# VectorE's score blocks move from matmuls of their own into the third bank of the score tiles

## The chip, the cores and the metric

The kernel runs on one core of one Trainium2 chip. TensorE (PE) multiplies matrices and writes only into PSUM, ScalarE (ACT) and VectorE (DVE) read PSUM and SBUF, GpSimd (POOL) copies a few small tiles, and SyncE (SP) issues DMAs. The metric is the device time of one execution in microseconds; the time of a kernel is the median of several executions. In addition one execution is profiled, and all rows quoted here come from such an execution.

## The reference

The kernel computes a gated sum of an attention block and a dense block over the same 2048 rows of 640 numbers:

```python
def _A_ref(x, wqkv, wo):            # H = 32 heads of Dh = 20
    qkv = (x @ wqkv).reshape(B, S, 3, H, Dh) ...
    scores = jnp.einsum("bhqd,bhkd->bhqk", q, k) * Dh ** -0.5
    p = softmax(scores, axis=-1)
    o = jnp.einsum("bhqk,bhkd->bhqd", p, v)
    return o.reshape(B, S, D) @ wo
def _B_ref(x, w1, b1, w2):          # F = 1536
    h = x @ w1 + b1
    return (h * jnp.tanh(softplus(h))) @ w2
g = sigmoid((x * gate_w).sum(-1, keepdims=True))
return g * _A_ref(x, ...) + (1 - g) * _B_ref(x, ...)
```

The large part is the exponential of 32 x 2048 x 2048 scores.

## The kernel before

**Units, groups, iterations.** Four heads and 512 queries form a group; there are 32 groups. A group has 16 blocks of 128 keys, and a block of one head is a unit: one matmul with 32 rows of contraction (20 are used) gives a tile of 128 keys x 512 queries, which is one PSUM bank. The four heads `t` of a unit row lie in four different strips of 32 rows of the array (`tile_position=(32 * t, 0)`). The list `units` is cut into iterations of three and two units in turn (`WIDTHS = (3, 2)`). An iteration has a PSUM tile, `S0` with three banks or `S1` with two, and each of them exists once: the scores of iteration i + 2 go into the tile that iteration i's exponential has read.

**One iteration.** `emit_qk` (line 1056 on) issues the score matmuls (line 1070), `emit_exp` one exponential on ScalarE over all banks of the tile (line 1081), `emit_pv` the sets of four matmuls that multiply finished exponentials with V and add up in the tile `acc` (line 1128). The scores of iteration i + 1 are issued ahead of the exponential of iteration i.

**Work beside it.** All other matmuls (projections of Q, K and V, both layers of the dense block, the output projection) are cut into "chains". A chain takes one of two further PSUM banks, the pool `pp`, runs its matmuls between the score bursts, and VectorE then copies the bank out (an eviction). `pump` chooses how many matmuls of chains fit between two bursts. It follows a planner's clock for every engine (the dictionary `T`), due times, and an estimate of TensorE's recent activity: where the estimate is below `FLOOR = 0.54` and a pool bank is free, it issues a matmul on constant data (`busy`, line 1014), which keeps TensorE occupied. The order of each engine's instructions is thereby fixed when the program is built.

**VectorE's share of the exponential.** In groups 4 to 30 the last block of keys (`JV`, block 15) is not among the units: VectorE computes its exponential by integer and polynomial steps. Four chains per group, one for each head `t`, come into the pool about 2 to 11 iterations after the group's start. Each has a single matmul (line 702), and its eviction (line 711) rounds 128 x 512 scores to 16-bit integers in `E_dve`. After the fourth, `jv_steps` computes on all four heads at once: seven instructions on 128 x 2048 elements (lines 730 to 752), each issued when the planner finds room on VectorE (`run_slow`). When they are done by the planner's clock, `emit_jv` issues the set of four matmuls that adds this block to `acc`.

ScalarE also computes 48 exponentials of 128 x 512 for the dense block (line 522). SyncE's and GpSimd's queues carry loads of weights and the outputs; none of them is issued by the chains that the change touches.

Of the kernel before, what the change touches and what calls it, by code (L numbers as in the profile page):

```python
# [9 lines left out]
P = 128  # L10
ACT = mybir.ActivationFunctionType
ALU = mybir.AluOpType
# [138 lines left out]
def kernel(  # L151
# [12 lines left out]
    nc = tc.nc  # L164
    _, S, D = A_x.shape
# [6 lines left out]
    QC = 512  # L172
# [6 lines left out]
    WIDTHS = (3, 2)  # L179
    JV_GROUPS = list(range(4, 31))  # L180
    JV_BIAS = 32
    LEAD_JV = 24
    N_CAP = 1.0e9
    NCELL = 48
    CELLS_KEPT = 2
# [41 lines left out]
    F16, I16 = mybir.dt.float16, mybir.dt.int16  # L227
    E_dve = consts.tile([P, 4, QC], BF16, tag="E_dve")
    w_dve = consts.tile([P, 4, QC], F16, tag="w_dve")
    VB = consts.tile([P, H, DH + 1], BF16, tag="VB")  # L230
    u_dve = consts.tile([P, 4, QC], F16, tag="u_dve")
# [39 lines left out]
    for c in range(1, NQC):  # L271
        nc.gpsimd.dma_start(  # L272
            out=xs[c][:, :, :],
# [5 lines left out]
        out=wv[:, :, GC : GC + 1], in_=gate_w.rearrange("(kt p o) -> p kt o", p=P, o=1)  # L279
# [16 lines left out]
    groups = [(p, qc) for p in range(NQ - 2) for qc in range(NQC)]  # L296
# [5 lines left out]
    JV = NS - 1  # L302
    with_jv = [G in JV_GROUPS for G in range(len(groups))]
# [5 lines left out]
        for t in range(4)  # L309
    ]  # L310
    unit_at = {(G, j): k for k, (G, _, _, j, t) in enumerate(units) if t == 0}
    iters = []
    pos = 0
    while pos < len(units):
        n = min(WIDTHS[len(iters) % len(WIDTHS)], len(units) - pos)
        iters.append((pos, n))
        pos += n
    NI = len(iters)
    it_of = [0] * len(units)
    for i, (a, n) in enumerate(iters):  # L320
# [3 lines left out]
    def it_at(G, j=0):  # L324
        return it_of[unit_at[(G, j)]] if G < len(groups) else NI

    kT = {}
    qT = {}
    OT = {}
    Bt = {}  # L330
    act = {}
# [12 lines left out]
    now = [0]  # L344
# [3 lines left out]
    T = dict(act=0.0, pe=0.0, dve=0.0, acc=0.0)  # L348
# [3 lines left out]
    NS_SEEN = 250.0  # L352
# [4 lines left out]
    def vec(ns, dep=0.0):  # L357
        T["dve"] = max(T["dve"], dep) + ns

    def evac(ns):  # L360

        run_slow(T["pe"] + NS_SEEN + 150.0)
        vec(ns, T["pe"] + NS_SEEN)
        bank_free[-1] = max(bank_free[-1], T["dve"] + 60.0)
# [31 lines left out]
    def steps(start, parts, deadline):  # L396


        seq[0] += 1
        slow.append([deadline, seq[0], start, deque(parts)])  # L400

    def run_slow(limit):

        while True:
            todo = [x for x in slow if max(T["dve"], x[2]) + x[3][0][0] <= limit]
            if not todo:
                break
            x = min(todo, key=lambda x: x[:2])
            ns, fn = x[3].popleft()
            vec(ns, x[2])  # L410
            fn()
            if not x[3]:
                slow.remove(x)
# [29 lines left out]
    def opener(box, *shape):  # L443
        def bank():
            if "ps" not in box:
                n = shape[0] * (shape[1] if len(shape) > 1 else 1)
                box["flat"] = take_bank()[:, 0:n]
                box["ps"] = box["flat"]
                if len(shape) > 1:
                    box["ps"] = box["flat"].rearrange("p (a b) -> p a b", b=shape[1])  # L450
            return box["flat"]

        return bank
# [238 lines left out]
    ROUND = 1.5 * 2.0**23  # L692
    jv_free = [True]
    jv_at = {}

    def jv_chain(G, p, t, start, due):
        box = {}
        bank = opener(box, QC)

        def piece():  # L700
            jv_free[0] = False
            nc.tensor.matmul(  # L702
                bank()[:, :],
                lhsT=kT[p][32 * t : 32 * t + 32, JV * P : (JV + 1) * P],
                rhs=qT[G][32 * t : 32 * t + 32, :],
                tile_position=(32 * t, 0),
            )

        def finish():
            evac(690)  # L710
            nc.vector.tensor_scalar(  # L711
                out=E_dve.bitcast(I16)[:, t, :], in0=box["ps"][:, :], scalar1=ROUND,
                scalar2=ROUND - 512.0 * JV_BIAS, op0=ALU.add, op1=ALU.subtract,
            )
            if t == 3:
                left = (it_at(G + 1) - now[0]) * 1115.0
                steps(T["dve"], jv_steps(G), T["act"] + left - 4000.0)

        def ready():
            return G in qT and (jv_free[0] if t == 0 else not jv_free[0])  # L720

        return Chain(start, due, [(215, piece)], finish, ready, hard=False, bank=bank, lead=LEAD_JV)

    def jv_steps(G):
        V = nc.vector
        E, w, u = (t.rearrange("p a n -> p (a n)") for t in (E_dve, w_dve, u_dve))
        e, wi = E.bitcast(I16), w.bitcast(I16)

        def mantissa():
            V.tensor_scalar(  # L730
                out=wi, in0=e, scalar1=511, scalar2=0x4000, op0=ALU.bitwise_and, op1=ALU.bitwise_or
            )

        def exponent():
            V.tensor_scalar(
                out=e, in0=e, scalar1=-512, scalar2=2, op0=ALU.bitwise_and, op1=ALU.logical_shift_right
            )

        def square():
            V.tensor_tensor(out=w, in0=w, in1=w, op=ALU.mult)  # L740

        def factor():
            V.tensor_scalar(out=u, in0=w, scalar1=EXP_A, scalar2=EXP_C, op0=ALU.add, op1=ALU.mult)

        def factor2():
            V.tensor_scalar(out=w, in0=w, scalar1=EXP_B, scalar2=None, op0=ALU.add)

        def product():
            V.tensor_tensor(out=w.bitcast(BF16), in0=w, in1=u, op=ALU.mult)

        def scale():
            V.tensor_tensor(out=e, in0=e, in1=wi, op=ALU.add)
            jv_at[G] = T["dve"] + NS_SEEN

        return [
            (700, mantissa), (700, exponent), (1230, square), (700, factor), (700, factor2),
            (1230, product), (1230, scale),
        ]


# [126 lines left out]
    for a in range(0, NS, 4):  # L887
        chains.append(
            v_chain(list(range(a, a + 4)), wv0, 0, 4 * DH, 0, 0, max(1, it_at(0, a)))
        )  # L890

    for G, (p, qc) in enumerate(groups):
        if with_jv[G]:
            for t in range(4):
                x = it_at(G) + 1 + 2 * t
                chains.append(jv_chain(G, p, t, x, x + 2))

    def spread(a, b, n):
        return [(a + (b - a) * k / n, a + (b - a) * (k + 1) / n) for k in range(n)]
# [152 lines left out]
    E_of = {}  # L1052
    S_free = {}
    S_full = {}
    E_full = {}
    late = [0.0]

    def emit_qk(i):
        a, n = iters[i]
        w = WIDTHS[i % len(WIDTHS)]  # L1060
        tag = f"S{i % len(WIDTHS)}"
        ps = spool.tile([P, w * QC], F32, tag=tag, name="Sp")
        S_of[i] = ps
        T["pe"] = max(T["pe"], S_free.get(tag, 0.0))
        S_full[i] = T["pe"] + NS_SCORES_SEEN
        worked(T["pe"], 215.0, 0.5)
        T["pe"] += NS_SCORES
        for k in range(n):
            G, p, qc, j, t = units[a + k]
            nc.tensor.matmul(  # L1070
                ps[:, k * QC : (k + 1) * QC],
                lhsT=kT[p][32 * t : 32 * t + 32, j * P : (j + 1) * P],
                rhs=qT[G][32 * t : 32 * t + 32, :],
                tile_position=(32 * t, 0),
            )

    def emit_exp(i):
        a, n = iters[i]
        which = i % len(WIDTHS)
        E = ep[which].tile([P, WIDTHS[which] * QC], BF16, tag=f"E{which}", name="E")  # L1080
        nc.scalar.activation(  # L1081
            E[:, 0 : n * QC], S_of.pop(i)[:, 0 : n * QC], ACT.Exp, scale=LN2 / 512.0
        )
        late[0] += max(0.0, S_full[i] - T["act"])
        T["act"] = max(T["act"], S_full.pop(i)) + NS_EXP[n]
        S_free[f"S{i % len(WIDTHS)}"] = T["act"] + NS_EXP_SEEN
        for k in range(n):
            E_of[a + k] = E[:, k * QC : (k + 1) * QC]
            E_full[a + k] = T["act"] + NS_EXP_SEEN
# [33 lines left out]
    def emit_set(G, p, qc, j, moving, full, VB=None):  # L1123
        n = pv_sets[0]
        T["pe"] = max(T["pe"], full, T["acc"] if n == 0 else 0.0) + NS_SET
        worked(T["pe"] - NS_SET, 215.0, 1.1)
        for t in range(4):
            nc.tensor.matmul(  # L1128
                acc[32 * t : 32 * t + DH + 1, :],
                lhsT=VA[:, j, 4 * p + t, :] if VB is None else VB[:, 4 * p + t, :],  # L1130
                rhs=moving(t),
                start=(n == 0),
                stop=(n == NS - 1),
                tile_position=(0, 32 * t),
            )
        pv_sets[0] = n + 1
        if n == NS - 1:
            normalise(G, p, qc)
            pv_sets[0] = 0
            jv_in[0] = False  # L1140

    def emit_jv(G, p, qc):
        jv_in[0] = jv_free[0] = True
        emit_set(G, p, qc, JV, lambda t: E_dve[:, t, :], jv_at[G], VB)

    def emit_pv(limit):
        count = 0
# [193 lines left out]
```

## Time and profile before

| | |
|---|---|
| median of 3 executions | 945.32 us (940.99 to 949.07) |
| the profiled execution | 954.2 us, of which the span of all instructions is 952.3 us |
| ScalarE busy | 912.2 us, 96% of the span |
| TensorE busy | 863.2 us, 91% |
| VectorE busy | 694.3 us, 73% |
| score matmuls (line 1070), exponentials (line 1081) | 1940, 776 |
| matmuls and evictions of VectorE's blocks (lines 702, 711) | 108 each |
| matmuls on constant data (line 1014) | 246 |
| granted TensorE clock, mean | 0.962 |

A line of the profile names the source line, the engine, the operation, what is written and what is read, how often, then the busy time of the group, the mean length of one, and the idle time of the engine just before it with the instruction that ended it. An instruction's length includes the time it takes to pass through the engine, so two instructions in a row overlap; how much an engine takes per instruction is read from the distance of the starts. "Granted clock" is the share of TensorE's full clock in that stretch; here it is 1 or 0.5.

### The profile page before, as it was taken

How to read it: one execution, taken by the hardware profiler on the slowest of the kernel's cores; microseconds unless marked ns; L12 is line 12 of the kernel's file. 1: busy time of each engine (PE TensorE's matmuls, PEld its weight loads, DVE VectorE, ACT ScalarE, POOL GpSimd, SP SyncE). 2: the span in 40 equal slices, each digit the busy share in tenths (PEclk: the TensorE clock that was granted, in tenths of full speed). 3: DMA queues.
4: the chain of work that ended last, by engine and by line, in shares of the span. 5: the costliest groups of instructions: out<-in, count | busy, mean ns of one | idle time of the engine just before them, and what ended most of it. 6: DMA issues, size and time to landing. Idle time of an engine off the chain costs nothing.

```text
span 952.3 us, 14757 instructions
## 1 busy us (share of the span) xinstructions
PE 863.2 (91%) x6073; PEld 298.8 (31%) x6073; DVE 694.3 (73%) x1156; ACT 912.2 (96%) x830; POOL 21.7 (2%) x35
## 2 busy tenths in 40 slices
PE   8999989999998888899899989898999899999996
PEld 4443322222233232322223222232223223333332
DVE  4335487777888888777788988788787877876533
ACT  6999998989999999989999999999999989999995
POOL 5000010000000000000000000000000000000000
PEclk9999997979999999979999999999999989999998
DMA  9000010000100010001011001010000000000100
GB/s 289 8 1 1 21 30 1 18 4 1 31 4 19 2 30 1 21 1 50 1 30 35 22 1 30 1 50 1 21 1 21 1 1 15 35 15 9 42 28 30
DMA packets 25632, 21.96 MB, mean 23 GB/s; under 512 B 10089, under 2 KB 24313, under 8 KB 25561
## 3 DMA queue, kind: packets, MB, share of 16 engines
q1 hardware_dynamic: 22808, 14.28, 5.5%
q0 software_dynamic: 1520, 5.94, 2.0%
q8 instruction: 48, 0.79, 0.3%
q10 hardware_dynamic: 1232, 0.76, 0.3%
q14 instruction: 24, 0.19, 0.1%
HBM read 15.73 MB, written 5.24 MB: 22 GB/s over the span
## 4 chain that ended last, share of the span: by engine, by line
ACT 61%; issue 18%; PE 18%; DVE 1%; DMA 1%; POOL 1%; ACTq 0%; POOLq 0%
ACT E L1081 58%; PE Sp L1070 5%; PE acc L1128 3%; ACT e L522 3%; PE ps L657 2%; PE ps L612 2%; PE ps L581 2%; PE ps L464 2%; DMA wv<-in_A_wqkv_dram 1%; PE ps L702 1%; PE ps L1014 0%; PE ps L492 0%; DVE ot L1291 0%; DVE h L592 0%; POOL xs L272 0%
## 5 line engine op out<-in xcount | busy, mean ns | idle before, releaser
L1081 ACT ACTIVATE E<-Sp 128x1536 bf16<-128x1536 f32 (+1 forms) x776 | 894.5, 1351 | 21.9 <-PE Sp L1070 20.8
L1070 PE MATMUL Sp<-qT,kT 32*128 32x512 bf16 x1940 | 313.2, 392 | 76.6 <-ACT E L1081 65.5
L1070 PEld LDWEIGHTS <-kT 32*128 32x128 bf16 x1940 | 104.0, 91 | 306.4 <-issue 287.9
L1128 PE MATMUL acc<-E,VA 128*21 128x512 bf16 x1940 | 196.6, 395 | 0.8 <-DVE T L1096 0.8
L1128 PEld LDWEIGHTS <-VA 128*21 128x21 bf16 x1940 | 47.8, 89 | 113.0 <-issue 112.7
L711 DVE TENSOR_SCALAR E_dve<-ps 128x512 int16<-128x512 f32 x108 | 71.8, 678 | 12.7 <-PE ps L702 12.3
L581 PE MATMUL ps<-xT,w1t 128*128 128x512 bf16 x240 | 80.3, 406 | 0.0
L1014 PE MATMUL ps<-busy 128*128 128x512 bf16 x246 | 75.5, 389 | 0.0
L612 PE MATMUL ps<-w_sb,cell 128*128 128x320 bf16 x384 | 75.3, 307 | 0.0
L592 DVE TENSOR_SCALAR h<-ps,b1f 128x512 f32<-128x512 f32 x48 | 35.8, 746 | 37.5 <-PE ps L581 37.2
L464 PE MATMUL ps<-xT,wkp 128*128 128x512 bf16 x155 | 49.1, 405 | 1.7 <-DVE xT L430 0.8
L464 PE MATMUL ps<-xT,wqp 128*128 128x512 bf16 x155 | 48.4, 392 | 0.0
L657 PE MATMUL ps<-wo_sb,cell 128*128 128x320 bf16 x248 | 46.9, 305 | 0.0
L544 DVE RECIPROCAL r<-r 128x128 f32<-128x128 f32 x48 | 45.4, 945 | 1.0
L479 DVE CAST kT<-ps 128x512 bf16<-128x512 f32 x31 | 21.4, 690 | 32.2 <-PE ps L464 32.1
L475 DVE TENSOR_SCALAR qT<-ps 128x512 bf16<-128x512 f32 x31 | 21.4, 692 | 27.1 <-PE ps L464 26.9
L612 PEld LDWEIGHTS <-cell 128*128 128x128 bf16 x384 | 30.0, 98 | 34.3 <-issue 27.6
L1096 DVE STREAM_TRANSPOSE T<-acc 128x512 f32<-128x512 f32 x32 | 22.9, 715 | 23.0 <-PE acc L1128 22.8
L702 PE MATMUL ps<-qT,kT 32*128 32x512 bf16 x108 | 38.3, 387 | 0.0
L522 ACT ACTIVATE e<-h 128x512 f32<-128x512 f32 x48 | 35.5, 739 | 0.7 <-DVE h L592 0.7
L505 DVE CAST VA<-ps 128x80 bf16<-128x80 f32 (+2 forms) x48 | 16.4, 378 | 25.0 <-PE ps L492 24.9
L553 DVE TENSOR_TENSOR e<-e,r 128x512 f32<-128x512 f32 x48 | 33.2, 692 | 1.6
(107 smaller groups left out, 694.3 us busy)
## 6 DMA issues: line engine op xcount, KB each, us to landing
w1t<-in_B_w_dram SPq DMA_DIRECT2D x14, 480.0 KB, 3.7
b_dram<-Bt SPq DMA_DIRECT2D x4, 640.0 KB, 3.1
out_dram<-ot SPq DMA_DIRECT2D x14, 160.0 KB, 1.8
xs<-in_A_x_dram POOLq DMA_DIRECT2D x3, 640.0 KB, 6.7
w_sb<-in_B_w_dram POOLq DMA_DIRECT2D x1, 1920.0 KB, 12.6
ws<-in_A_wqkv_dram SPq DMA_DIRECT2D x13, 100.0 KB, 3.9
w1t<-in_B_w_dram POOLq DMA_DIRECT2D x2, 480.0 KB, 8.8
wo_sb<-in_A_wo_dram SPq DMA_DIRECT2D x4, 200.0 KB
```

The source lines that it names most:

```text
L464: nc.tensor.matmul(box["ps"][:, :], lhsT=wpad[:, kt, :, :].rearrange("p h d -> p (h d)"), rhs=xT[:, kt, chunk * QC : (chunk + 1) * QC], st ...
L522: nc.scalar.activation(e[:, :], h[:, :], ACT.Exp)
L544: V.reciprocal(out=r[:, Q], in_=r[:, Q])
L581: nc.tensor.matmul(box["ps"][:, :], lhsT=w1t[4 * c + ft // 3][:, kt, (ft % 3) * P : (ft % 3 + 1) * P], rhs=xT[:, kt, c * QC : (c + 1) * QC ...
L612: nc.tensor.matmul(box["ps"][:, :], lhsT=act[(ft, c)][:, u * P : (u + 1) * P], rhs=w2_sb[:, ft, half * HALF : (half + 1) * HALF], start=(f ...
L657: nc.tensor.matmul(box["ps"][:, :], lhsT=OT[(p, c)][:, u * P : (u + 1) * P], rhs=wo_sb[0][:, p, cols], start=(k == 0), stop=(k == len(ps_l ...
L702: nc.tensor.matmul(bank()[:, :], lhsT=kT[p][32 * t : 32 * t + 32, JV * P : (JV + 1) * P], rhs=qT[G][32 * t : 32 * t + 32, :], tile_positio ...
L711: nc.vector.tensor_scalar(out=E_dve.bitcast(I16)[:, t, :], in0=box["ps"][:, :], scalar1=ROUND, scalar2=ROUND - 512.0 * JV_BIAS, op0=ALU.ad ...
L1014: nc.tensor.matmul(ps[:, 0:n], lhsT=busy[:, :], rhs=busy_row(n), start=True, stop=True)
L1070: nc.tensor.matmul(ps[:, k * QC : (k + 1) * QC], lhsT=kT[p][32 * t : 32 * t + 32, j * P : (j + 1) * P], rhs=qT[G][32 * t : 32 * t + 32, :] ...
L1081: nc.scalar.activation(E[:, 0 : n * QC], S_of.pop(i)[:, 0 : n * QC], ACT.Exp, scale=LN2 / 512.0)
L1128: nc.tensor.matmul(acc[32 * t : 32 * t + DH + 1, :], lhsT=VA[:, j, 4 * p + t, :] if VB is None else VB[:, 4 * p + t, :], rhs=moving(t), st ...
```

## The change

VectorE's blocks lose their chains and their pool banks. When the list of units is cut into iterations, four iterations of each group 4 to 30 that would have three units get two, and the third bank of their `S0` tile takes a block of VectorE's (`extra`). The first comes at least 4 iterations after the group's start, the others 2, 4 and 2 iterations later (`JV_GAPS`). `emit_qk` issues that matmul as the third of the burst and directly behind it, through `jv_read`, VectorE's rounding read of this bank. `emit_exp` covers the first two banks. The planner's clock lets `S0` come free only when both the exponential and VectorE's read are through. A 3-bank iteration takes the head whose strip of the array is not used by its two units if one is left.

The steps of VectorE's exponential are issued twice per group, each time on 128 x 1024 elements: after the second and after the fourth read. The set that adds the block to `acc` comes when both halves are done.

```diff
-    LEAD_JV = 24
+    JV_GAPS = (4, 2, 4, 2)
...
+        x = None
+        got = taken_by.setdefault(G, [])
+        if with_jv[G] and n == 3 and len(got) < 4:
+            since = i - (got[-1][0] if got else iters_start.get(G, i))
+            if since >= JV_GAPS[len(got)] and units[pos + 1][0] == G:
+                mine = {units[pos][4], units[pos + 1][4]}
+                left = [t for t in range(4) if t not in [y for _, y in got]]
+                t = min(left, key=lambda t: (t in mine, t))
+                got.append((i, t))
+                x = (G, units[pos][1], t, len(got) - 1)
+                n = 2
...
-    def jv_chain(G, p, t, start, due):
...
+    def jv_read(G, t, slot, ps, full):
+        assert jv_free[0] or slot > 0
+        jv_free[0] = False
+        jv_slot[t] = slot
+        run_slow(full + 100.0)
+        vec(690, full)
+        nc.vector.tensor_scalar(
+            out=E_dve.bitcast(I16)[:, slot, :], in0=ps, scalar1=ROUND,
+            scalar2=ROUND - 512.0 * JV_BIAS, op0=ALU.add, op1=ALU.subtract,
+        )
+        if slot % 2 == 1:
+            left = (it_at(G + 1) - now[0]) * 1115.0
+            steps(T["dve"], jv_steps(G, slot // 2), T["act"] + left - 4000.0)
...
-            (700, mantissa), (700, exponent), (1230, square), (700, factor), (700, factor2),
-            (1230, product), (1230, scale),
+            (380, mantissa), (380, exponent), (640, square), (380, factor), (380, factor2),
+            (640, product), (640, scale),
...
-    for G, (p, qc) in enumerate(groups):
-        if with_jv[G]:
-            for t in range(4):
-                x = it_at(G) + 1 + 2 * t
-                chains.append(jv_chain(G, p, t, x, x + 2))
...
+        todo = [(units[a + k][0], units[a + k][1], units[a + k][3], units[a + k][4]) for k in range(n)]
+        if extra[i] is not None:
+            G, p, t, slot = extra[i]
+            todo.append((G, p, JV, t))
+        for k, (G, p, j, t) in enumerate(todo):
             nc.tensor.matmul(
                 ps[:, k * QC : (k + 1) * QC],
...
+        if extra[i] is not None:
+            jv_read(G, t, slot, ps[:, n * QC : (n + 1) * QC], S_full[i])
+            S_read[i] = T["dve"] + 60.0
...
+        if i in S_read:
+            S_free[tag] = max(S_free[tag], S_read.pop(i))
```

More of the change, by code (lines that the diff above doesn't have):

```diff
@@ L312 @@
     iters = []
+    extra = []
     pos = 0
+    taken_by, iters_start = {}, {}
     while pos < len(units):
-        n = min(WIDTHS[len(iters) % len(WIDTHS)], len(units) - pos)
+        i = len(iters)
+        G = units[pos][0]
+        n = min(WIDTHS[i % len(WIDTHS)], len(units) - pos)
+        x = None
[9 more added lines that the diff above has]
+                n = 2
+        for k in range(pos, pos + n):
+            iters_start.setdefault(units[k][0], i)
         iters.append((pos, n))
+        extra.append(x)
         pos += n
+    assert all(len(taken_by[G]) == 4 for G in JV_GROUPS)
     NI = len(iters)
@@ L694, with jv_steps @@
     jv_at = {}
-    def jv_chain(G, p, t, start, due):
[L697 to L724, printed above, removed]
+    jv_slot = {}
+    halves = {}
+    def jv_read(G, t, slot, ps, full):
[11 more added lines that the diff above has]
+            steps(T["dve"], jv_steps(G, slot // 2), T["act"] + left - 4000.0)
+    def jv_steps(G, half):
         V = nc.vector
-        E, w, u = (t.rearrange("p a n -> p (a n)") for t in (E_dve, w_dve, u_dve))
+        E, w, u = (
+            t[:, 2 * half : 2 * half + 2, :].rearrange("p a n -> p (a n)")
+            for t in (E_dve, w_dve, u_dve)
+        )
         e, wi = E.bitcast(I16), w.bitcast(I16)
@@ L752, in scale @@
             V.tensor_tensor(out=e, in0=e, in1=wi, op=ALU.add)
-            jv_at[G] = T["dve"] + NS_SEEN
+            halves[G] = halves.get(G, 0) + 1
+            if halves[G] == 2:
+                jv_at[G] = T["dve"] + NS_SEEN
         return [
-            (700, mantissa), (700, exponent), (1230, square), (700, factor), (700, factor2),
-            (1230, product), (1230, scale),
+            (380, mantissa), (380, exponent), (640, square), (380, factor), (380, factor2),
+            (640, product), (640, scale),
         ]
@@ L1054 @@
     S_full = {}
+    S_read = {}
     E_full = {}
@@ L1067, in emit_qk @@
         T["pe"] += NS_SCORES
-        for k in range(n):
-            G, p, qc, j, t = units[a + k]
+        todo = [(units[a + k][0], units[a + k][1], units[a + k][3], units[a + k][4]) for k in range(n)]
[3 more added lines that the diff above has]
+        for k, (G, p, j, t) in enumerate(todo):
             nc.tensor.matmul(
@@ L1085, in emit_exp @@
         T["act"] = max(T["act"], S_full.pop(i)) + NS_EXP[n]
-        S_free[f"S{i % len(WIDTHS)}"] = T["act"] + NS_EXP_SEEN
+        tag = f"S{i % len(WIDTHS)}"
+        S_free[tag] = T["act"] + NS_EXP_SEEN
+        if i in S_read:
+            S_free[tag] = max(S_free[tag], S_read.pop(i))
         for k in range(n):
@@ L1143, in emit_jv @@
         jv_in[0] = jv_free[0] = True
-        emit_set(G, p, qc, JV, lambda t: E_dve[:, t, :], jv_at[G], VB)
+        emit_set(G, p, qc, JV, lambda t: E_dve[:, jv_slot[t], :], jv_at[G], VB)
     def emit_pv(limit):
```

## The prediction, on record before the changed kernel ran

> **What bounds the kernel now.** I read the page first: busy times, granted clock, costliest groups.
>
> ```profile
> PE 863.2 (91%) x6073; PEld 298.8 (31%) x6073; DVE 694.3 (73%) x1156; ACT 912.2 (96%) x830; POOL 21.7 (2%) x35
> ...
> PEclk9999997979999999979999999999999989999998
> ...
> L1070 PE MATMUL Sp<-qT,kT 32*128 32x512 bf16 x1940 | 313.2, 392 | 76.6 <-ACT E L1081 65.5
> ...
> L711 DVE TENSOR_SCALAR E_dve<-ps 128x512 int16<-128x512 f32 x108 | 71.8, 678 | 12.7 <-PE ps L702 12.3
> ```
>
> ScalarE is busy 96% of the span. TensorE's score matmuls wait 65.5 us for ScalarE to release their tile. VectorE's eviction of a block takes 678 ns. The clock has dents. Next, the groups with shapes kept apart:
>
> ```profile
> L1081 ACT ACTIVATE E<-Sp 128x1536 bf16<-128x1536 f32 x388 | 607.8, 1567 | 6.4 <-PE Sp L1070 5.8
> L1081 ACT ACTIVATE E<-Sp 128x1024 bf16<-128x1024 f32 x388 | 440.6, 1136 | 15.5 <-PE Sp L1070 15.0
> ```
>
> These lengths overlap. In the trace's starts, the instruction after a three-bank exponential comes 1330 ns later, after a two-bank one 904, after one for the dense block 519 (each both minimum and median). So 388 x 1.330 + 388 x 0.904 + 48 x 0.519 = 891.7 us of the span is ScalarE at its rate. The first exponential starts at 10.4 us, 11.3 us lie behind the last, and the remainder, 38.8 us, is lateness of exponentials. Where does that lie? I put the half-clock stretches into a table of windows: all engines first, then line 702 alone. Columns: length, busy time and number of instructions by engine, clock, DMA share, GB/s.
>
> ```profile
> 138.47:155.54 17.07, 16.03 (x73) 3.82 (x72) 11.34 (x19) 12.95 (x11) 0.00 (x0) 0.50 0.08 16
> 155.54:172.61 17.07, 15.37 (x108) 4.61 (x106) 13.90 (x22) 16.89 (x17) 0.00 (x0) 1.00 0.00 0
> ...
> 432.02:435.43 3.41, 2.55 (x15) 0.69 (x15) 2.69 (x5) 3.41 (x4) 0.00 (x0) 1.00 0.00 0
> 435.43:438.85 3.42, 3.19 (x15) 1.03 (x14) 2.00 (x5) 2.44 (x3) 0.00 (x0) 0.50 0.00 0
> ```
>
> ```profile
> 432.02:435.43 3.41, 1.14 (x3) 0.28 (x3) 1.00 0.00 0
> 435.43:438.85 3.42, 0.00 (x0) 0.00 (x0) 0.50 0.00 0
> ```
>
> At half clock ScalarE does 11 instructions where it does 17 at full clock. Nine half-clock stretches lie between 138 and 784 us, 61 us in all; 25.0 of the 38.8 us of lateness lie in them and the 3.5 us behind each. They are multiples of 3.41 us long on one grid. Cutting 40 to 940 us on that grid, full-clock cells with no matmul of line 702 number 173, and none is followed by half clock; with one, 45 and none; with two or three, 27, and all nine. The timeline shows why these cells are thin:
>
> ```profile
> 550.59 0.52 PE L702 MATMUL ps<-qT,kT 32*128 32x512 bf16 x2
> ...
> 550.85 0.47 PE L1070 MATMUL Sp<-qT,kT 32*128 32x512 bf16 x2
> 551.01 1.29 DVE L711 TENSOR_SCALAR E_dve<-ps 128x512 int16<-128x512 f32 x2 [0.33 <-PE ps L702]
> 552.19 0.39 PE L1070 MATMUL Sp<-qT,kT 32*128 32x512 bf16 x3 [0.87 <-ACT E L1081]
> ```
>
> Two blocks of VectorE's hold both pool banks until 552.3, and TensorE has nothing to put in: a hole of 0.87 us.
>
> **The change part by part.** *Shorter iterations.* 1940 units make 819 iterations in place of 776: 302 of three banks, 517 of two. 302 x 1.330 + 517 x 0.904 = 869.0 us against 866.8: +2.2.
>
> *A wait on ScalarE.* The built instruction order of the changed kernel shows something that the source doesn't say: 108 of the 819 exponentials, those of the iterations with a VectorE block, wait for VectorE's semaphore, at the count that `jv_read` of the same tile raises. Before, none of 776 waits for VectorE. Read and exponential take different banks of one tile, and are ordered one behind the other. Behind the waiting exponential stand all later ones; the V sets wait for its output, and the next score burst of this tile for its end. The planner's clock doesn't know this wait.
>
> Its price: the read ends after lag + 680 ns from the end of the scores (line 711, median). In before's 108 blocks the lag from matmul to read is 37 ns at least, 189 median, 246 mean, 627 at the ninth tenth. The shortest steps from VectorE's end to a waiting exponential of line 522 are 33 ns. Without the wait the exponential would start by ScalarE's rate: for three-bank tiles the scores are ready 207 ns earlier (median; a tenth under 47). With TensorE in time it is 904 - 557 = 347, since a burst's end never comes earlier than 557 ns after the release. So the exponential is late by lag + 680 + 33 - headstart: at best 37 + 713 - 347 = 403 ns, by before's mean lag and median headstart 246 + 713 - 207 = 752. The late exponentials give TensorE and VectorE time to catch up, which shortens the lag and brings the headstart near 347: I take a lag of 150 (nearer the median than the mean) and a headstart of 317 (nearer 347 than 207): 150 + 713 - 317 = 546, nearer to the lower end. Times 108: **+59 us, bounds 44 and 81**.
>
> The Trainium skill has a rule that speaks for the change: "PSUM — Partial Sum Buffer", section "PSUM bank collisions raise a hardware error", has VectorE and ScalarE on different banks at once without error. By it alone the wait would be needless and this term 0; the built order has it all the same.
>
> *The third matmul.* 81 of the 108 blocks have a strip of their own beside the two units; 27 share one. A block's matmul directly ahead of a burst (399.02 us) put its start off by 0.18 us (399.20 us): 27 x 0.18 = +5, bounds 0 and 5; I take 4.
>
> *What leaves the pool.* 108 matmuls and 108 banks' occupation go; the 43 further bursts take some 0.32 us each (distance to the next matmul) beside ScalarE's work. TensorE's matmuls on constant data rise from 246 to 350 in the built order, so the planner finds free banks more often. By the grid above the nine half-clock stretches lose their cause: down to -25.
>
> *What thins TensorE anew.* Two late exponentials lie two iterations apart: 3 x 0.904 us of ScalarE's rate take 2.71 + 2 x 0.55 = 3.8 us, and TensorE's work, placed for 2.71, spreads over it. The grid cells ahead of half clock held 2.4 to 2.9 us of TensorE's busy time in 3.41; the mean of the span is 0.91 x 3.41 = 3.1; 3.1 x 2.71/3.8 = 2.2 falls below. So the 54 pairs can each start a half-clock stretch; with cells on a fixed grid I take 20, at the 1.4 us of lateness of the short ones (1.3 to 1.8): 28 us, bounds 0 and 54 x 1.4 = 76, no longer than that since line 1070's wait leaves TensorE time to catch up. Against the 25 that go: +3.
>
> For the clock the trace has drops behind cells in which TensorE was busy 70% and more. The Trainium skill ("TensorE: Matmul & The Clock Gate", section "Part 1: The HAM clock gate") halves the clock after an idle window of some 3.4 us; the trace doesn't bear out that it takes an idle one. By the rule no pair would trigger it and this term would be -25.
>
> *VectorE.* Fixed cost: 256 against 128 elements of the dense block's products take 425 and 292 ns, so some 159 ns each are fixed. Halves add 7 x 159 = 1.1 us per group, 30 us in all, beside 258 us of VectorE's idle time: 0 here, bounds 0 and the lag above. The old condition for a free `S0` (read before exponential's end) falls away, since the exponential now starts behind the read. No DMA, POOL or SP instruction moves relative to the scores.
>
> Sum: 2.2 + 59 + 4 + 3 = +68, less the few us of lateness behind thin slack (13.8 us before outside the stretches), which the pauses absorb: I take 3. **+65**. The profiled execution goes from 954.2 to 1019. It stands 9 us above the median run; I add 65 to the median: **1010 us**.
>
> **Rivals.** *Cheap wait, clock healed* (0.13): the read always starts at once, TensorE is in time, no half clock: 945 + 2 + 44 - 25 = 966, to 985. For: 350 matmuls on constant data. Against: VectorE's queue has before's lags.
>
> *Clock spreads* (0.20): most pairs halve the clock, and the wait stays near its upper bound: 945 + 2 + 75 + 5 + 25 = 1052, 1035 to 1080.
>
> *Not slower, the wait doesn't bind* (0.05): the exponential's wait at `jv_read` is met before ScalarE is free. It decides from a headstart of lag + 713 = 750 ns on; before, a tenth of the three-bank tiles had over 629, and the most was 878. Price: 2 + 4 - 25 = -19, 926 us.
>
> *The change doesn't do what it says*: in the built order a read that stands beside the exponential in the source stands ahead of it; that is the forecast itself.
>
> **How the numbers follow.** The forecast, 985 to 1035, has 0.62. The range leaves out the last rival, a little of the first and the second's upper part: 968 (wait at 44, clock at -25, rest +4) to 1055. A measurement here can tell about 1%, 9.5 us. Faster by more: 0.03; within: 0.02; slower: 0.95.
>
> **What would show it.** Right: exponentials idle for VectorE some 108 times, 400 to 750 ns each; two-bank exponentials x517; line 702's group gone; half-clock cells behind pairs of reads. Wrong: idle time in the exponential's group put down to TensorE instead, or no idle time; a clock at 1 throughout takes 28 us from the sum, half clock over more than 150 us adds to it.

## The result, and the profile after

The changed kernel takes **992.5 us** (median of 4, 983.7 to 995.2) against 944.6 us (median of 4, 941.0 to 949.1): a ratio of **1.049**, 95% interval 1.041 to 1.057. It is slower, as forecast (1010, range 968 to 1055), by 48 us where 65 were forecast. The profiled execution takes 993.2 us, with a span of 991.4; before it was 954.2 and 952.3.

The page of the changed kernel (busy times, granted clock, and from the costliest groups the exponentials, the score bursts, VectorE's reads and the matmuls on constant data):

```profile
PE 887.2 (89%) x6177; PEld 309.5 (31%) x6177; DVE 720.7 (73%) x1345; ACT 922.1 (93%) x873; POOL 22.4 (2%) x35
...
PEclk9999999999999999999799999999999997899998
...
L1097 ACT ACTIVATE E<-Sp 128x1024 bf16<-128x1024 f32 (+1 forms) x819 | 902.6, 1250 | 51.8 <-DVE E_dve L726 40.2
L1083 PE MATMUL Sp<-qT,kT 32*128 32x512 bf16 x2048 | 331.0, 388 | 90.9 <-ACT E L1097 78.3
...
L726 DVE TENSOR_SCALAR E_dve<-Sp 128x512 int16<-128x512 f32 x108 | 74.7, 691 | 61.7 <-PE Sp L1083 61.3
L1023 PE MATMUL ps<-busy 128*128 128x512 bf16 (+1 forms) x350 | 110.4, 391 | 0.0
```

ScalarE was the bound and is now busy 93% of a longer span. Its exponentials stand idle 51.8 us, 40.2 of them behind an instruction that no exponential waited for before: `jv_read`'s rounding read, line 726. Kept apart by shape, all of that lies ahead of two-bank exponentials:

```profile
L1097 ACT ACTIVATE E<-Sp 128x1024 bf16<-128x1024 f32 x517 | 547.3, 1080 | 47.5 <-DVE E_dve L726 40.2 <-PE acc L1147 4.2 <-PE Sp L1083 2.7
L1097 ACT ACTIVATE E<-Sp 128x1536 bf16<-128x1536 f32 x302 | 465.0, 1540 | 4.4 <-PE Sp L1083 4.2
```

The answer on who waited for whom (total, times, longest) gives the same pair, and shows that VectorE for its part waits for the scores:

```profile
DVE E_dve L726 <- PE Sp L1083: 61.3, 90, 1.7
ACT E L1097 <- DVE E_dve L726: 40.2, 100, 1.5
```

One such step in the timeline: the burst of three starts at 686.26, the read takes 686.70 to 687.39, and the exponential starts at 687.43.

```profile
686.26 0.39 PE L1083 MATMUL Sp<-qT,kT 32*128 32x512 bf16 x3
...
686.70 0.69 DVE L726 TENSOR_SCALAR E_dve<-Sp 128x512 int16<-128x512 f32 x1
...
687.43 1.02 ACT L1097 ACTIVATE E<-Sp 128x1024 bf16<-128x1024 f32 x1 [0.30 <-DVE E_dve L726]
```

Idle time understates the loss, because consecutive exponentials overlap: 40.2 us of idle time are 57.3 us of lateness when measured from start to start, as in the prediction. With that measure both profiled spans come apart (rounded to 0.1 us):

| us | before | after |
|---|---|---|
| up to the first exponential | 10.4 | 10.2 |
| ScalarE at its rate | 891.7 | 893.9 |
| lateness of the 108 exponentials behind VectorE's reads | - | 57.3 |
| lateness elsewhere, in and just behind half-clock stretches | 25.0 | 11.9 |
| lateness elsewhere, the rest | 13.9 | 6.9 |
| behind ScalarE's last exponential, at its rate | 11.3 | 11.2 |
| span | 952.3 | 991.4 |

So +57.3 for the wait, -13.1 and -7.0 for the rest of the lateness, +2.2 for shorter iterations. Between the medians the difference is 48 and not 39, since before's profiled execution, at 954.2 us, was longer than each of the executions timed.

### The profile page after: what moved, and what is told of

Same layout as the page of the kernel before. It is cut to its first block, busy times and chain, and to the rows that moved or that the text cites. A ratio compares the mean times of both kernels' runs of the same rounds, so it can differ in the third digit from the quotient of the medians.

```text
span 991.4 us, 15219 instructions
## 1 busy us (share of the span) xinstructions
PE 887.2 (89%) x6177; PEld 309.5 (31%) x6177; DVE 720.7 (73%) x1345; ACT 922.1 (93%) x873; POOL 22.4 (2%) x35
## 4 chain that ended last, share of the span: by engine, by line
ACT 56%; issue 17%; PE 16%; DVE 9%; DMA 1%; POOL 1%; POOLq 0%; ACTq 0%
ACT E L1097 53%; PE Sp L1083 8%; DVE E_dve L726 7%; ACT e L543 3%; PE acc L1147 2%; PE ps L633 1%; PE ps L485 1%; PE ps L602 1%; PE ps L678 1%; PE ps L1023 1%; DMA wv<-in_A_wqkv_dram 1%; DVE ot L1310 0%; DVE h L613 0%; DVE qT L496 0%; POOL xs L272 0%
## 5 line engine op out<-in xcount | busy, mean ns | idle before, releaser
L1097 ACT ACTIVATE E<-Sp 128x1024 bf16<-128x1024 f32 (+1 forms) x819 | 902.6, 1250 | 51.8 <-DVE E_dve L726 40.2
L1083 PE MATMUL Sp<-qT,kT 32*128 32x512 bf16 x2048 | 331.0, 388 | 90.9 <-ACT E L1097 78.3
L1083 PEld LDWEIGHTS <-kT 32*128 32x128 bf16 x2048 | 113.8, 91 | 338.3 <-issue 317.0
L726 DVE TENSOR_SCALAR E_dve<-Sp 128x512 int16<-128x512 f32 x108 | 74.7, 691 | 61.7 <-PE Sp L1083 61.3
L1023 PE MATMUL ps<-busy 128*128 128x512 bf16 (+1 forms) x350 | 110.4, 391 | 0.0
L1023 PEld LDWEIGHTS <-busy 128*128 128x128 bf16 x350 | 27.0, 98 | 44.1 <-issue 35.7
L551 DVE SCALAR_TENSOR_TENSOR e<-e 128x512 f32<-128x512 f32 x48 | 32.8, 684 | 10.6 <-ACT e L543 10.6
L762 DVE TENSOR_TENSOR w_dve<-w_dve,u_dve 128x1024 bf16<-128x1024 f16 x54 | 37.0, 686 | 0.8
L765 DVE TENSOR_TENSOR E_dve<-E_dve,w_dve 128x1024 int16<-128x1024 int16 x54 | 36.6, 685 | 1.0
L753 DVE TENSOR_TENSOR w_dve<-w_dve 128x1024 f16<-128x1024 f16 x54 | 36.7, 680 | 0.0
```

The costliest lines, as they stand in the source:

```text
L726: nc.vector.tensor_scalar(out=E_dve.bitcast(I16)[:, slot, :], in0=ps, scalar1=ROUND, scalar2=ROUND - 512.0 * JV_BIAS, op0=ALU.add, op1=ALU ...
L1023: nc.tensor.matmul(ps[:, 0:n], lhsT=busy[:, :], rhs=busy_row(n), start=True, stop=True)
L1083: nc.tensor.matmul(ps[:, k * QC : (k + 1) * QC], lhsT=kT[p][32 * t : 32 * t + 32, j * P : (j + 1) * P], rhs=qT[G][32 * t : 32 * t + 32, :] ...
L1097: nc.scalar.activation(E[:, 0 : n * QC], S_of.pop(i)[:, 0 : n * QC], ACT.Exp, scale=LN2 / 512.0)
```

## The experiments

All in all eight kernels ran, each against the kernel before on the same chip. Their expectations were on record before they ran.

**The block in a bank of its own.** The matmul stays the third of a short burst, but writes a pool bank:

```diff
+        if extra[i] is not None:
+            xb = take_bank()
...
-                ps[:, k * QC : (k + 1) * QC],
+                ps[:, k * QC : (k + 1) * QC] if k < n else xb[:, :],
...
-            jv_read(G, t, slot, ps[:, n * QC : (n + 1) * QC], S_full[i])
-            S_read[i] = T["dve"] + 60.0
+            jv_read(G, t, slot, xb[:, :], S_full[i])
+            bank_free[-1] = max(bank_free[-1], T["dve"] + 60.0)
```

> The changed kernel, but the block's matmul, still issued as the third of the burst, writes a pool bank of its own instead of the tile's third bank; iterations as short as in the changed kernel, steps in halves. No exponential waits for VectorE in the built order. Theory (the exponential's wait for VectorE's read is the cost): 57 us of lateness go, against 2.2 us for shorter iterations that stay, and the pool banks held by VectorE's reads can bring half-clock stretches back: 935 to 955 us, exponentials idle for VectorE about 0. Rival (the shorter iterations, or VectorE's doubled number of steps, are the cost): it stays at 980 to 995.

Measured: 948.6 us, ratio to before 1.005 (1.000 to 1.010). With iterations as short as in the changed kernel, and the halved steps, 43 of its 48 us are gone; the cost is the shared tile. No exponential's wait is put down to VectorE's read, and lateness is 29.3 us in all: the 57.3 us behind the reads went, and 10.5 us came up elsewhere (29.3 against 18.8). One part of the expectation failed: the half-clock stretches did not come back (none before 936 us). What the exponentials wait for is TensorE's bursts and V sets:

```profile
ACT E L1099 <- PE Sp L1085: 6.2, 15, 0.9
ACT E L1099 <- PE acc L1149: 4.0, 9, 0.8
```

**Half a read.**

```diff
-            out=E_dve.bitcast(I16)[:, slot, :], in0=ps, scalar1=ROUND,
+            out=E_dve.bitcast(I16)[:, slot, 0:256], in0=ps[:, 0:256], scalar1=ROUND,
```

(`E_dve` is cleared once, at 57.5 us, which takes 0.9 us.)

> The changed kernel with VectorE reading 256 of the 512 columns of each block (half of each of VectorE's blocks is left out of the result, the steps run on all columns as before). Theory (each exponential is late by lag + read - headstart): the read goes from 691 to about 425 ns, 108 x 0.27 = 29 us less: 955 to 970 us, lateness about 270 to 290 ns per block. Rival (the wait is covered and the cost sits in TensorE's bursts or the clock): within 8 us of the changed kernel's 992.

Measured: 955.8 us, ratio 1.015 (1.011 to 1.018). The read takes 425 ns in place of 691, and the exponentials behind it are late by 268 ns on the mean instead of 530: 28.9 us in all against 57.3. The dose answers one to one. The time fell by 37 us and not by 29, because lateness elsewhere fell too, from 18.8 to 8.4 us: this run has no half clock before its last 11 us.

```profile
ACT E L1097 <- DVE E_dve L726: 10.2, 34, 1.2
```

**Only the steps in halves, in the kernel before.**

```diff
-            if t == 3:
+            if t % 2 == 1:
...
-                steps(T["dve"], jv_steps(G), T["act"] + left - 4000.0)
+                steps(T["dve"], jv_steps(G, t // 2), T["act"] + left - 4000.0)
```

with `jv_steps` on 128 x 1024 elements as in the change.

> The kernel before with one part of the change alone: VectorE's steps in halves, after the second and the fourth block; blocks in the pool as before. Theory (VectorE's 1.1 us more per group is hidden by its idle time): within 1% of before, 938 to 952 us. Rival (VectorE's work is on the path): VectorE's lag grows and holds pool banks longer, 955 us or more with more half clock than 61 us.

Measured: 938.9 us, ratio 0.996 (0.993 to 0.999). VectorE's additional 189 instructions cost nothing; this part alone is a gain at the edge of what can be told. Half clock inside the profiled run is 17 us, against 65 in before's (64.8 by the clock's records; the prediction and the expectations say 61). But before's profiled execution is an extreme one. Its mean clock is 0.962; the 15 executions of the kernel before that ran beside this kernel have 0.962 to 0.985, median 0.978, and this kernel's ten have 0.976 to 0.988, median 0.987. So halves alone save less half clock than 65 against 17 says.

**The two readers in the other order.**

```diff
-        if extra[i] is not None:
-            jv_read(G, t, slot, ps[:, n * QC : (n + 1) * QC], S_full[i])
-            S_read[i] = T["dve"] + 60.0
...
-        if i in S_read:
-            S_free[tag] = max(S_free[tag], S_read.pop(i))
+        if extra[i] is not None:
+            G, p, t, slot = extra[i]
+            jv_read(G, t, slot, Sp[:, n * QC : (n + 1) * QC], S_free[tag])
+            S_free[tag] = T["dve"] + 60.0
```

> The changed kernel with VectorE's read issued behind the exponential of the same tile: in the built order the read waits for the exponential, and no exponential for VectorE. Theory (the order of the two readers only moves the wait: the tile comes free 0.7 us later and the next burst into it is late): release at 0.12 + 0.03 + 0.69 = 0.85 us after the next exponential's start, then some 0.5 us for the burst, against 0.90: 0.4 to 0.5 us late, times 108 = 43 to 54: 980 to 1000 us, with the lateness now behind TensorE's scores of the iteration two later. Rival (the tile's hold is covered, only the direct wait costs): 930 to 950.

Measured: 983.8 us, ratio 1.043 (1.040 to 1.047). The exponential no longer waits for the read, the read waits for the exponential, and the tile's next burst for the read:

```profile
PE Sp L1083 <- DVE E_dve L726: 58.7, 105, 1.2
DVE E_dve L726 <- ACT E L1095: 54.2, 77, 2.3
```

The next exponential that starts behind a read is late by 478 ns on the mean, 51.6 us in all, within the 0.4 to 0.5 us expected. The cost moves and stays: in one tile with one copy, the two reads stand one behind the other whichever is first.

**Reads further apart.** `JV_GAPS = (6, 4, 4, 4)` in place of `(4, 2, 4, 2)`.

> The changed kernel with its four reads 6, 4, 4 and 4 iterations apart instead of 4, 2, 4, 2, so that no two late exponentials fall into one 3.4 us cell. Theory (pairs of waits thin TensorE's work and start the half-clock stretches; the wait itself is the same): lateness at the reads stays at 53 to 60 us, the six half-clock stretches inside go to 0 or 1, which is worth up to 12 us: 978 to 990 us. Rival (the stretches have another cause, such as single waits): six or so stay, 990 to 995.

Measured: 981.7 us, ratio 1.037 (1.032 to 1.043). The wait is what it was (54.0 us, 500 ns each); half clock inside the run falls from 44 to 10 us, lateness elsewhere from 18.8 to 11.2. The clock of all four executions agrees: 0.988 to 0.994, where the changed kernel's four have 0.970 to 0.987. Of the three stretches left, two follow cells in which no read starts, so pairs of reads aren't the only cause. In one of these cells (before 823.8 us) TensorE stands 1.25 us for VectorE's `top_b`, in the other (before 885.3 us) 0.9 us for VectorE's last step and 0.8 us for its transposition of `acc`.

**A fourth matmul in full iterations.** As in the first experiment, but `n = 2` is left out, so the iteration keeps its three units, and the block's head is taken from the strip that the three units leave free. That holds for 81 of the 108 blocks; by the code, the last head of each of the 27 groups shares a strip with one of the three units:

```diff
-            if since >= JV_GAPS[len(got)] and units[pos + 1][0] == G:
-                mine = {units[pos][4], units[pos + 1][4]}
+            if since >= JV_GAPS[len(got)] and units[pos + 2][0] == G:
+                mine = {units[pos + k][4] for k in range(3)}
...
-                n = 2
```

> The block's matmul goes as a fourth into three-unit iterations, in the strip of the array that their three units leave free, and into a pool bank of its own; iterations as long as in the kernel before, steps in halves. Theory (an exponential over three banks costs nothing more, and without the shared tile no exponential waits for VectorE): ScalarE's rate 891.7 us as before, but bursts that find their pool bank held, as with the bank of its own in short iterations (18 us of lateness there): 940 to 950 us. Rival (four matmuls in four strips and a bank taken early free TensorE and end the half-clock stretches without new lateness): 925 to 938.

Measured: **935.6 us** (935.2 to 936.4), ratio **0.989** (0.984 to 0.994): the rival's range held, and this is faster than both kernels, by 1.1% against the kernel before. A part of this is the steps in halves, which alone gave 0.996. There is no half clock until the tail, and lateness is 20.2 us in all.

```profile
PE 859.4 (92%) x6211; PEld 303.5 (33%) x6211; DVE 717.0 (77%) x1345; ACT 910.1 (97%) x830; POOL 21.8 (2%) x35
...
PEclk9999999999999999999999999999999999999998
```

**The blocks further apart in the pool of the kernel before**, with the steps in halves: `x = it_at(G) + 1 + 4 * t`, `LEAD_JV = 0`; and `1 + 3 * t` with the lead of 24.

> The kernel before with VectorE's steps in halves and the four blocks of a group due 4 iterations apart in the pool (1, 5, 9 and 13 after the group's start) instead of 2, without their lead in the order of chains. Theory (the half-clock stretches of the kernel before come from two or three blocks in one 3.4 us cell of the pool): cells with two or more blocks become rare, half clock inside the run goes from 61 us to under 15, lateness falls by 10 to 20 us: 922 to 938 us. Rival (the stretches come from VectorE's or ScalarE's load, not from the blocks' places): half clock as before, 938 to 950.

> As the run before it, with the blocks due 3 iterations apart and with their lead of 24 in the order of chains as in the kernel before. Theory: between the halves alone (939 us) and the spacing of 4: 925 to 940 us, half clock inside the run under 17 us. Rival: half clock as before, 938 to 950.

Measured: 945.9 us, ratio 1.001 (0.998 to 1.003), for 4 apart; 937.2 us, ratio 0.991 (0.988 to 0.994), for 3 apart. Both have less half clock inside (13.7 and 10.2 us; the halves alone have 17). With 4 apart, and without the lead, the blocks come so late that in two groups VectorE isn't through when the group's sum needs them. Chosen lines of that run's timeline:

```profile
898.10 0.39 PE L1134 MATMUL acc<-E_dve,VB 128*21 128x512 bf16 x2
...
900.59 0.69 DVE L756 TENSOR_TENSOR E_dve<-E_dve,w_dve 128x1024 int16<-128x1024 int16 x1
901.33 0.39 PE L1134 MATMUL acc<-E_dve,VB 128*21 128x512 bf16 x2 [2.83 <-DVE E_dve L756]
```

TensorE stands 2.83 us for VectorE's last step, and the 6.8 us at half clock from 901.7 us on follow. The other such wait (1.91 us, at 868.4 us) has a half-clock stretch behind it too. The lateness from 1 us before to 3 us behind these two waits is 6.9 us, and in all this run has 7.9 us more lateness than the run with 3 apart (28.7 against 20.8). So the expectation of 922 to 938 failed for this kernel by a new wait. Two things were changed at once here, the distance and the lead; which of them makes the blocks late was not separated.

## Why the prediction was right, and by how much its terms were off

*The wait on ScalarE* (+59, bounds 44 and 81): **+57.3**. The mechanism read from the built order is what the trace shows, and three interventions agree: without the shared tile it goes, with 266 ns less of the read it falls by 262 ns a block, with the order turned it moves to the bursts. Inside the term two sizes were off against each other. The read starts 55 ns behind the scores on the mean (median 42), where I took 150: VectorE is early and waits for the scores 90 times. The headstart was 252 ns, where I took 317. 55 + 691 + 36 - 252 = 530 against my 546: that the sum came so close is in part luck. The four reads of a group differ, as the argument from catching up said: the first is late by 684 ns (headstart 119), the others by 422, 475 and 540 (headstart 345, 320, 223).

*Shorter iterations* (+2.2): +2.2 by the rates; the first experiment contains this part, and is some 5 us above before with it.

*The third matmul* (+4): about +3, and it lies inside the 57.3. The 27 blocks that share a strip with a unit are the fourth reads of their groups. In their bursts the third matmul starts 215 ns behind the first, in the other 81 it starts 9 ns behind it, and the burst ends 587 ns after its start instead of 394 (medians at full clock). The second reads also close a pair, but have a strip of their own. Against them the fourth are late by 540 ns instead of 422, and 27 x 118 ns is 3.2 us.

*What leaves the pool, what thins TensorE anew* (25 us go, 28 come, +3): **25.0 went, 11.9 came, -13**. This is the step that failed in size. I let 20 of the 54 pairs of waits start a half-clock stretch; six stretches were in the trace (44 us). Where five of them begin (24 us, 6.7 of the 11.9 us of lateness) fits the argument: each begins 0.7 to 1.6 us after the start of an exponential that had waited for the second read of a pair. The sixth, the longest with 20.5 us and 5.2 us of lateness, does not. It begins 0.5 us after an exponential behind a first read, and in the cell ahead of it TensorE stands 1.25 us for VectorE's `top_b`, in a small chain that runs once and bounds the size of the scores. The kernel before has no such wait, and the prediction had no term for it. Whether the hole or the read started this stretch was not tested. Two tables of windows, the second for VectorE's reads alone (length, VectorE's busy time, clock, DMA share, GB/s), then the hole:

```profile
472.73:476.14 3.41, 2.54 (x15) 0.68 (x15) 2.21 (x5) 2.61 (x3) 0.00 (x0) 1.00 0.00 0
476.14:486.38 10.24, 9.84 (x41) 1.95 (x44) 8.03 (x15) 7.62 (x8) 0.00 (x0) 0.50 0.00 0
...
827.72:831.13 3.41, 2.16 (x19) 0.66 (x18) 2.34 (x7) 1.95 (x3) 0.00 (x0) 1.00 0.00 0
831.13:851.61 20.48, 20.48 (x91) 5.02 (x87) 11.01 (x25) 13.76 (x13) 0.00 (x0) 0.50 0.03 9
```

```profile
472.73:476.14 3.41, 0.97 (x2) 1.00 0.00 0
476.14:486.38 10.24, 0.00 (x0) 0.50 0.00 0
```

```profile
829.20 0.34 PE L858 MATMUL ps<-ident,top_b 128*32 128x128 bf16 x3 [1.25 <-DVE top_b L854]
```

In the cells ahead of half clock TensorE was busy 2.2 to 2.5 of 3.41 us, near the 2.2 that I worked out for a pair. Seven other full-clock cells of the changed kernel lie in the same range (2.18 to 2.54 us) and no half clock follows them. So TensorE's busy time alone, as the trace has it, doesn't tell which cell starts a stretch, and why these six did I have not settled. That the 104 more matmuls on constant data kept other cells busier was not tested.

The -25 has a fault of its own: I read it from the profiled execution, whose 65 us at half clock are much for this kernel, and added the sum to the median. The 38 executions of the kernel before that were timed beside the experiments have a mean clock of 0.962 to 0.988, median 0.976, and the profiled one has 0.962; the changed kernel's profiled execution, with 0.974, lies among its other three (0.970, 0.975, 0.987). An estimate from these figures: at 0.976 some 45 us of before's span are at half clock, less about 8 in the tail 37, and at 25.0/64.8 us of lateness each that is 14 us. Between typical executions the term is then near -2, not -13. My +3 is close to that by luck, since both its parts were about twice too large.

*Thin slack* (-3): -7.0, from 13.9 to 6.9 us.

By terms, my 2.2 + 59 + 4 + 3 - 3 = 65 became 2.2 + 57.3 (the third matmul's 3.2 among them) - 13.1 - 7.0 = 39.4 in the profiled spans. With -2 in place of -13.1 it is about 50, and between the medians 48 were measured.

The claim that half clock in the kernel before comes from VectorE's blocks bunching in the pool gained support: with the blocks in the bursts in a bank of their own, at unchanged or shorter iterations, no stretch is left inside the run, and spacing them by 3 leaves 10 us. It is not the whole cause: the halved steps alone, with the blocks' spacing as it was, have 17 us in their profiled execution, and the clock of their ten executions (median 0.987) lies above before's. Cells with two or three blocks still headed all five stretches there.

That two readers on different banks must stand one behind the other was not tested on the chip without the wait: the built order has it for both orders of issue, and only another tile removed it. The Trainium skill's page ("PSUM — Partial Sum Buffer", section "PSUM bank collisions raise a hardware error") doesn't require it for different banks; the first and the sixth experiment, where ScalarE and VectorE read different tiles, show nothing against that, and no run here shows two readers at once in one tile.

## What to carry to other kernels

Look at the waits in the built order, not at the source, when an instruction gets a second reader on another engine: two reads of one PSUM tile were put one behind the other, and VectorE's read of 691 ns made the bound engine late at 105 of 108 exponentials, by 530 ns on the mean of all. A block that only another engine needs belongs into a tile of its own; where three heads leave a strip of the array free, its matmul can still go with their burst. That version has the lowest median here (935.6 us), though the blocks 3 apart in the pool (937.2, from 933.9 to 943.6) can't be told from it. Blocks that hold a pool bank for 0.7 us of reading but give TensorE one matmul headed the half-clock stretches where they came in twos and threes; what spacing them by 3 is worth by itself is small (0.991 against 0.996 with the halves alone, intervals that touch).

## What the runs showed of the hardware that I had not expected

A fourth matmul in a free strip costs TensorE almost nothing, and one in a taken strip costs 0.2 us. Both can be seen in the run with four matmuls:

```profile
170.34 0.39 PE L1084 MATMUL Sp<-qT,kT 32*128 32x512 bf16 x3
170.35 0.38 PE L1084 MATMUL ps<-qT,kT 32*128 32x512 bf16 x1
...
172.60 0.39 PE L1084 MATMUL Sp<-qT,kT 32*128 32x512 bf16 x3
172.83 0.37 PE L1084 MATMUL ps<-qT,kT 32*128 32x512 bf16 x1
```

Of the 81 blocks with a strip of their own, 68 start 9 to 20 ns behind the first of their three units. The next matmul follows 327 ns after the burst's start (median of the 81), against 324 behind bursts of three. The other 13 start 0.2 to 0.8 us late, each 52 to 54 ns after VectorE has emptied a pool bank. The 27 that share a strip start 228 to 233 ns behind the first, and the next matmul follows at 538 ns. With this and 384 matmuls on constant data the clock stays full to the end of the loop.

The spread between executions goes with the clock. The kernel with four matmuls has 0.997 in all four of its executions, and they lie within 1.2 us of one another. The kernel before spreads over 14 us in 23 executions. For the changed kernel's four, 0.970 goes with 995.2 us, 0.974 with 993.2, 0.975 with 991.8, 0.987 with 983.7; for the 38 of the kernel before, the ends are 0.962 with 953.7 us and 0.988 with 939.5, and in between longer executions have the lower clock nearly throughout. So most of the spread between executions of one kernel here goes with how much half clock each happened to get. Why one execution gets more of it than another, no run shows.
